# Block-sorted attention and a gated MLP on one core: chunk 2's queries and two units of chunk 1 transposed by DMA, a new order for the first two chunks

## The chip, the cores and the metric

The kernel runs on one core of a Trainium2 chip. The core has five engines that run side by side: TensorE (PE, matrix products, with its weight loads shown as PEld), VectorE (DVE), ScalarE (ACT), GpSimd (POOL) and SyncE (SP, which here only issues DMAs). Sixteen DMA engines move data between the memory of the chip and the core's own memory, and inside the latter. DMAs are put into queues by SP, ACT and POOL; loads that change the type from f32 to bf16 are issued by POOL here. Results of PE go to PSUM, a small memory of banks, and are copied out of it ("evicted") by DVE or ACT.

The metric is device time in microseconds (us), the median of several executions. One execution was recorded by the profiler; its span is the time from its first to its last instruction.

## The reference

For each of 4 batches and 8 heads, a net of 8x8 numbers is normalized five times by rows and columns, and its result mixes the 8 blocks (96 rows each) of keys and values. Each block of 96 queries then attends to the mixed block of keys at its place. The attention output is reshaped to 3072 tokens of 512 numbers and goes through a two-layer MLP with the gate `h * cos(h)`.

```
for _ in range(5):
    P = exp(P - max(P, -1));  P = P / (sum(P, -1) + 1e-9);  P = P / (sum(P, -2) + 1e-9)
k_sorted = einsum('bhij,bhjcd->bhicd', P, k_blocks)      # 8 blocks of 96 rows, 64 wide
v_sorted = einsum('bhij,bhjcd->bhicd', P, v_blocks)
scores = (q_block @ k_sorted_block.T) / 8
attn = exp(scores - max);  attn = attn / (sum(attn) + 1e-9)
x = (attn @ v_sorted_block).transpose(0, 2, 1, 3).reshape(3072, 512)
h = x @ w_in                                             # 512 -> 2048
out = (h * cos(h)) @ w_out                               # 2048 -> 512
```

Inputs and output are f32; the products run in bf16.

## The kernel before

The tokens are worked in 8 **chunks** of 384: chunk n is batch n // 2 and one half (4 of 8 blocks) of its rows. A chunk has 4 **units**, one for each block of 96 rows; a unit is all 8 heads of it. Two batches make a **group**: chunks 0 to 3 are group 0, chunks 4 to 7 group 1.

A unit (n, u) goes through these steps. PE makes the scores of 8 heads (`s_ps` in chunks 0 and 1, `qk_products` later); DVE takes the maximum and subtracts it (`s_max`, `s_sub`, later `qk_reduce`); ACT takes the exponential into one of three buffers `p_buf` (`expo`). The probabilities are transposed into `pT` in one of two ways: with `on_pe=True` by 8 transposes on PE into PSUM (`p_ps`, name `pps`, L776) and a copy out of it (`p_ev`), without it by one DMA transpose that SP issues (L533). PE multiplies by the values (`av_products`), DVE divides by the sum (`av_norm`), and the result is transposed into `xT` (`x_ps`, `x_ev`). Then come the MLP's first product, the gate and the second product: for chunk 0 `up_four`, `cos_four`, `gate_four` and quarters `down_four` of 4 matmuls (names `h`, `c`, `gg`, `o`), from chunk 1 on `up` and `down`.

Ahead of the units, the keys and values are mixed on PE by block matrices `bds` and `bdv` made from the normalized net. Chunk 0's keys come from `kp`, the rest of group 0 from `ks`/`kse` (6 parts of 8 columns), group 1's from `k_sort_g` out of the tile `pair`. Half of the keys is needed on the other 64 partitions too: `k_swap` exchanges the halves by two DMAs of SP (L421, L422), for group 0 after the last `kse`, for group 1 after the last `k_next`. The scores of chunk 2 and of chunk 4 wait for it. The values are read through a copy `vperm` with permuted columns, made by POOL (`v_permute`, four instructions, L179), which needs all of the values' loads.

Queries come in two forms. For chunks below `NQ = 3` one load (L119) brings 4 rows at a time, PE transposes them (`q_products`, name `qps`, L268: 16 transposes for each half of the heads) and DVE or ACT places them in `q_turned`; rows of x then stand in another order, which `x_transpose` undoes with `order`. From chunk `NQ` on, eight small loads (L129) bring them into a tile with zeros between the heads (`zeros_between`, L137), `q_mem` for even chunks and a part of `kv` for odd ones, and two DMA transposes of SP turn them (`q_transpose_dma`, L149).

The order on every engine is the order in which the program is written, so the list of calls behind `k_next` and `w_two` (L845 and below) decides it by hand, engine by engine; an engine that waits holds up all that stands behind it. POOL issues the loads and also does the permutations and zeros; with some loads it waits first: `hold_keys` waits for the exchange of the keys, `p_hold(2, 2)` for a transposed `pT`. POOL's loads use eight completion semaphores in turn, so a ninth load waits for the first to land. SP issues stores, exchanges and transposes in the order of the list. Some functions take `fill`: so many matmuls of zeros that keep PE busy and whose result is overwritten.

Around the end of chunk 1 the list reads (L1036 to L1052, some calls left out):

```
    ks(1, *B)
    ...
    kse(1, A)
    k_swap(kT[1])
    q_transpose(2, 0, (V, V), *C)
    q_transpose(2, 1, (V, V), *B)
    zeros_between(3)
    load_q(3)
    hold_keys()
    load_pair(vbuf, vin_d, 0 * CD // 6, 1 * CD // 6)
    ...
    up(1, 0)
    v_sort_b(1, 0, 8, A, *C)
```

## Time and profile before

| | |
|---|---|
| median of 3 runs | 236.1 us (234.94 to 236.75) |
| the profiled execution, its own time | 235.54 us |
| its span, first to last instruction | 233.6 us, 1.9 us less than its time |
| PE busy | 224.1 us (96% of the span) |
| VectorE, ScalarE, GpSimd busy | 171.0, 154.4, 95.9 us |
| granted clock of PE | 1.00 throughout |
| moved by DMA | 31.19 MB in 67672 packets |

A row of the view in order of time has the start and the length in us, the engine, the line, the operation, the tiles as out<-in, the sizes and the count, and in brackets the idle time of the engine before it with what ended it. Matmuls are pipelined and their ends are modelled, so the time of a group is better read from the starts of neighbouring rows. A row of DMA issues has the tiles, the queue that issued, the count, the KB of one and the median time from issue to landing in us. A row of windows has the stretch and its length, the busy time of PE, PEld, DVE, ACT and POOL with counts, the granted clock, the DMA engines' busy share and the GB/s that they wrote.

### The profile page before, as it was taken

What the parts mean: (1) busy time and instruction counts of PE and PEld (TensorE: products, weight loads), DVE (VectorE), ACT (ScalarE), POOL (GpSimd) and SP (SyncE); (2) the same over time, 40 slices, a digit from 0 to 9 for tenths busy, and PEclk for the clock granted to TensorE, in tenths of its full rate; (3) what the DMA queues carried; (4) which work ended last, traced back from release to release, by engine and by line L of the source; (5) the groups of instructions that cost most, each with busy time, mean ns of one, the idle gap of its engine ahead of it and who ended that gap; (6) DMA issues with size and microseconds to landing.
All of it is one profiled execution on the core that took longest, in us unless ns stands there. A gap on an engine that the chain in (4) does not pass through costs nothing.

```text
span 233.6 us, 5420 instructions
## 1 busy us (share of the span) xinstructions
PE 224.1 (96%) x2212; PEld 141.8 (61%) x2212; DVE 171.0 (73%) x291; ACT 154.4 (66%) x209; POOL 95.9 (41%) x121
## 2 busy tenths in 40 slices
PE   8778999999999999998999999999999999999994
PEld 3367899567665656655666546655665566556553
DVE  6769867987789867885498885997699769745700
ACT  5648886776889758795788565655665566816621
POOL 7999999399950093992609002600000000000000
PEclk9999999999999999999999999999999999999999
DMA  5999999993999799898999679934933360351012
GB/s 73 227 190 206 203 206 227 204 223 124 124 134 175 123 166 151 130 198 134 139 145 101 96 99 195 170 65 88 177 128 64 73 186 0 68 144 45 3 45 90
DMA packets 67672, 31.19 MB, mean 134 GB/s; under 512 B 56384, under 2 KB 63168, under 8 KB 67392
## 3 DMA queue, kind: packets, MB, share of 16 engines
q0 software_dynamic: 24048, 13.64, 43.3%
q1 hardware_dynamic: 43312, 17.02, 35.1%
q8 instruction: 17, 0.28, 0.5%
q10 hardware_dynamic: 288, 0.20, 0.3%
q14 instruction: 7, 0.06, 0.1%
HBM read 27.27 MB, written 6.29 MB: 144 GB/s over the span
## 4 chain that ended last, share of the span: by engine, by line
PE 82%; DMA 8%; DVE 3%; POOL 3%; ACT 1%; issue 1%; SPq 0%; ACTq 0%; DVEq 0%; POOLq 0%
PE h L614 30%; PE o L639 27%; DMA kv<-in_v_dram 5%; PE h L798 5%; PE o L819 4%; PE sc L438 4%; PE av L570 3%; POOL vperm L179 3%; DMA pT<-p_buf 2%; PE ks L408 2%; PE o L1167 2%; DMA kTs<-kTs 1%; DVE xn L583 1%; PE vs L458 1%; PE pps L776 1%
## 5 line engine op out<-in xcount | busy, mean ns | idle before, releaser
L614 PE MATMUL h<-xT,w_in_t 128*128 128x384 bf16 x448 | 78.4, 326 | 0.0
L639 PE MATMUL o<-w_out_t,gg 128*128 128x512 bf16 x320 | 76.3, 379 | 0.0
L622 DVE TENSOR_TENSOR gg<-c,h 128x768 bf16<-128x768 f32 x56 | 52.7, 949 | 19.5 <-ACT c L618 19.4
L618 ACT ACTIVATE c<-h,half_pi 128x768 f32<-128x768 f32 x56 | 50.4, 900 | 24.5 <-PE h L614 23.6
L614 PEld LDWEIGHTS <-w_in_t 128*128 128x128 bf16 x448 | 42.2, 98 | 26.3 <-DVE xT L259 0.3
L639 PEld LDWEIGHTS <-gg 128*128 128x128 bf16 x320 | 29.1, 99 | 27.8
L515 ACT ACTIVATE p_buf<-s 96x768 bf16<-96x768 f32 x32 | 26.7, 842 | 5.6 <-DVE s L489 4.7
L179 POOL COPY vperm<-kv 64x768 bf16<-64x768 bf16 (+2 forms) x12 | 28.4, 2408 | 4.4 <-DMA kv<-in_v_dram 4.4
L489 DVE TENSOR_TENSOR s<-sc,mx 96x384 f32<-96x384 f32 (+1 forms) x33 | 24.3, 736 | 1.6
L487 DVE TENSOR_REDUCE mx<-sc 96x4 f32<-96x384 f32 (+1 forms) x33 | 24.0, 728 | 0.0
L583 DVE TENSOR_TENSOR xn<-av,r 96x512 bf16<-96x512 f32 x32 | 22.0, 687 | 1.1
L129 POOL DMA_DIRECT2D kv<-in_q_dram x24 | 16.0, 677 | 0.8 <-issue 0.5
L438 PE MATMUL sc<-kTs,q_turned 128*128 128x96 bf16 x224 | 15.4, 206 | 0.3 <-DMA kTs<-kTs 0.3
L257 ACT CAST kTs<-ks 128x512 bf16<-128x512 f32 x20 | 11.3, 582 | 6.3 <-PE ks L408 5.3
L581 DVE RECIPROCAL r<-av 96x8 f32<-96x8 f32 x32 | 6.4, 199 | 12.0 <-PE av L570 11.8
L438 PEld LDWEIGHTS <-q_turned 128*128 128x128 bf16 x224 | 12.6, 98 | 4.0 <-DVE s L489 0.6
L257 ACT COPY kv<-o 128x512 f32<-128x512 f32 (+2 forms) x10 | 5.2, 523 | 14.1 <-PE o L639 11.5
L129 POOL DMA_DIRECT2D q_mem<-in_q_dram x16 | 10.7, 690 | 4.6 <-DMA kv<-in_v_dram 4.2
L819 PE MATMUL o<-w_out_t,gg 128*128 128x512 bf16 x48 | 11.7, 379 | 0.0
L259 DVE COPY kv<-o 128x512 f32<-128x512 f32 (+1 forms) x5 | 3.1, 611 | 11.1 <-PE o L1167 8.5
L798 PE MATMUL h<-xT,w_in_t 128*128 128x192 bf16 x128 | 11.1, 246 | 0.0
L798 PEld LDWEIGHTS <-w_in_t 128*128 128x128 bf16 x128 | 10.5, 98 | 0.0
(128 smaller groups left out, 276.9 us busy)
## 6 DMA issues: line engine op xcount, KB each, us to landing
out_dram<-kv SPq DMA_DIRECT2D x12, 256.0 KB, 2.6
out_dram<-o_s SPq DMA_DIRECT2D x10, 256.0 KB, 3.7
w_in_t<-in_moe_w_in_dram POOLq DMA_DIRECT2D x4, 512.0 KB, 11.6
w_out_t<-in_moe_w_out_dram POOLq DMA_DIRECT2D x4, 512.0 KB, 12.6
kv<-in_k_dram POOLq DMA_DIRECT2D x2, 768.0 KB, 10.0
kv<-in_v_dram POOLq DMA_DIRECT2D x2, 768.0 KB, 13.3
pair<-in_k_dram POOLq DMA_DIRECT2D x2, 768.0 KB, 12.3
kv<-in_v_dram POOLq DMA_DIRECT2D x6, 256.0 KB, 5.6
```

Source lines behind the costliest of these rows:

```text
L129: nc.gpsimd.dma_start(out=q_heads[:, i, :, e], in_=src[:, ih * IC + i, :, e])
L179: nc.gpsimd.tensor_copy(dst, src)
L438: nc.tensor.matmul(out, q_of(n, hp)[:, x:x + 128], keys_of(n, u, h2, hp), start=True, stop=True)
L487: nc.vector.reduce_max(mx[:], scv, axis=AX.X)
L489: nc.vector.tensor_tensor(s, scv, mx.to_broadcast(list(s.shape)), op=ALU.subtract)
L515: nc.scalar.activation(p[:, :, :blk], s_t.pop((n, u)).rearrange("p e h c -> p (e h) c"), AF.Exp, scale=scale)
L583: nc.vector.tensor_tensor(xn.rearrange("p h e d -> p e h d"), avv[:, :, :, :D], r.to_broadcast([blk, 2, H2, D]), op=ALU.mult)
L614: nc.tensor.matmul(h[:, f2, :w], w_in_t[:, kk, f * 128:(f + 1) * 128], xT[n][:, kk], start=(kk == 0), stop=(kk == KC - 1))
L618: nc.scalar.activation(c[:], h[:, :, :w], AF.Sin, bias=half_pi[:, 0:1])
L622: nc.vector.tensor_tensor(gt[n, fp // 2][:, f:f + 2], c[:], h[:, :, :w], op=ALU.mult)
L639: nc.tensor.matmul(o[:], gt[n, f // 4][:, f % 4, ts * 128:(ts + 1) * 128], w_out_t[:, f, :], start=(f == 0), stop=(f == FC - 1))
L798: nc.tensor.matmul(o[:, part, f2 * w:(f2 + 1) * w], w_in_t[:, kk, f * 128:(f + 1) * 128], xT[0][:, kk, h * w:(h + 1) * w], start=(kk == 0) ...
```

## The change

Four things are changed, all in one list of calls.

- `NQ` is 2 instead of 3. Chunk 2's queries come by the eight small loads into `q_mem` and are turned by two DMA transposes; their 32 transposes on PE and four copies on DVE go. The zeros in `q_mem` are now laid for chunk 2 (`zeros_between(2)`) instead of chunk 4, whose call goes, as does `z_turned(0)`. Chunk 2's rows of x are in plain order. The place of `pT` for unit 0 of chunks 3 and 4 is kept by writing the numbers 3 and 4.
- Units (1, 1) and (1, 0) have `expo` without `on_pe`: SP transposes their probabilities, and two `p_ps` and `p_ev` go.
- The two loads of `pair` stand behind three of the four permutations of the second batch's values. `hold_keys` and the first three of six loads of group 1's values move behind `p_hold(2, 2)`, next to the other three.
- The order of the first two chunks is written anew: the first stage's key and value products, the fills, chunk 0's `down_four` behind those of the token tiles 1 and 2, the key parts `ks` spread through chunk 1 with `ks(0)` last, and the load of the sine table (`sine_next`) ahead of chunk 1's `up`.

```diff
-    QR, NQ = 4, 3
+    QR, NQ = 4, 2
...
-        if u == 0 and n in (NQ, NQ + 1):
+        if u == 0 and n in (3, 4):
...
+    q_products(1, 0, 0, 16, *C)
+    zeros_between(2)
+    cos_four(1, 0)
+    load_q(2)
...
+    v_permute(slice(64, 128), hi=48)
     load_pair(pair, kin_d, 0 * CD // 2, 1 * CD // 2)
     load_pair(pair, kin_d, 1 * CD // 2, 2 * CD // 2)
-    v_permute(slice(64, 128))
+    v_permute(slice(64, 128), 48)
...
+    expo(1, 1)
...
+    expo(1, 0)
...
+    q_transpose_dma(2)
...
+    ks(0, *B)
     down_four(0, 2)
...
+    kse(0, V)
+    k_swap(kT[1])
     x_ev(1, 1, A)
+    sine_next()
     x_ps(1, 0, *B)
     x_ps(1, 3, *B)
...
+    down_four(0, 3)
+    down_out(0, A)
     zeros_between(3)
     load_q(3)
-    hold_keys()
-    load_pair(vbuf, vin_d, 0 * CD // 6, 1 * CD // 6)
-    load_pair(vbuf, vin_d, 1 * CD // 6, 2 * CD // 6)
-    load_pair(vbuf, vin_d, 2 * CD // 6, 3 * CD // 6)
...
-    zeros_between(4)
...
     p_hold(2, 2)
-    for z in range(3, 6):
+    hold_keys()
+    for z in range(6):
         load_pair(vbuf, vin_d, z * CD // 6, (z + 1) * CD // 6)
     load_q(4)
```

What stands on POOL between chunk 0 and the loads of chunk 3's queries, before (`pair` are group 1's keys, `kv<-in_q_dram` chunk 3's queries, `vperm<-kv` the permutation of the second batch's values):

```order
L685 MEMSET p_buf_108 96x8x32
L685 MEMSET p_buf_109 96x8x32
L119 DMA q_mem<-in_q_dram 96x8x256
L92 DMA pair<-in_k_dram 128x3072 x2
L179 COPY vperm<-kv 64x1536 x4
L137 MEMSET kv 96x16x64 x2
L129 DMA kv<-in_q_dram 96x4x64 x8
```

The same place on POOL after the change:

```order
L685 MEMSET p_buf_108 96x8x32
L685 MEMSET p_buf_109 96x8x32
L137 MEMSET q_mem 96x16x64 x2
L129 DMA q_mem<-in_q_dram 96x4x64 x8
L179 COPY vperm<-kv 64x1536 x3
L92 DMA pair<-in_k_dram 128x3072 x2
L179 COPY vperm<-kv 64x1536
L137 MEMSET kv 96x16x64 x2
L129 DMA kv<-in_q_dram 96x4x64 x8
```

The one query load has become two memsets and eight loads, and the pair loads stand behind three permutations instead of ahead of all four.

SP from the start of the program to the transposes of chunk 3's queries (`q_turned_95<-kv`), before; the exchange of the keys is the pair L421 and L422:

```order
L81 DMA P<-in_sort_net_dram 32x64
L629 DMA out_dram<-o_s 128x512 x2
L629 DMA out_dram<-c 128x512
L421 DMA kTs<-kTs 64x1536
L422 DMA kTs<-kTs 64x1536
L149 DMA_TRANSPOSE q_turned_95<-kv 128x16x96 x2
```

And after:

```order
L81 DMA P<-in_sort_net_dram 32x64
L533 DMA_TRANSPOSE pT<-p_buf_108 128x8x96
L629 DMA out_dram<-o_s 128x512
L533 DMA_TRANSPOSE pT<-p_buf_107 128x8x96
L149 DMA_TRANSPOSE q_turned_94<-q_mem 128x16x96 x2
L629 DMA out_dram<-c 128x512
L421 DMA kTs<-kTs 64x1536
L422 DMA kTs<-kTs 64x1536
L629 DMA out_dram<-o_s 128x512
L149 DMA_TRANSPOSE q_turned_95<-kv 128x16x96 x2
```

Four transposes have come in ahead of the exchange, and one store has moved behind it.

POOL at the loads of group 1's values, after the change (`kv<-in_v_dram` are the values, `q_mem<-in_q_dram` chunk 4's queries); before, the cast from `kTs` and three of the loads stood far ahead, behind chunk 3's queries:

```order
L541 CAST held<-pT 96x1
L426 CAST held<-kTs 128x1
L92 DMA kv<-in_v_dram 128x1024 x6
L129 DMA q_mem<-in_q_dram 96x4x64 x8
L179 COPY vperm<-kv 128x1536 x4
```

All six value loads now follow one another, and chunk 4's query loads and the permutation come behind them.

More of the change, by code (lines that the diff above doesn't have):

```diff
@@ L843, in w_two @@
         next(wz)
-    kp(2, *B)
-    kp(0, *B)
+    kp(2, *B, fill=1)
+    blocks.append(block([pick[:, :, z * PB:(z + 1) * PB] for z in (1, 0)]))
     v_permute(slice(0, 64), 32, False, 8, 40)
@@ L850 @@
     v_permute(slice(0, 64), 56, False, 8, 64)
-    k_place(2, A, 1)
-    k_place(2, V, 0)
+    k_place(2, A, 0)
+    k_place(2, V, 1)
     kp(1, *B)
+    values_matrix()
+    kp(0, *B)
+    k_place(1, V, 0)
+    v0(0, *C)
     k_place(0, A, 0)
-    blocks.append(block([pick[:, :, z * PB:(z + 1) * PB] for z in (1, 0)]))
-    k_place(1, V, 0)
-    k_place(1, A, 1)
-    values_matrix()
+    k_place(1, V, 1)
+    s_ps(0, 0)
+    v0e(0, A)
+    s_max(0, 0)
+    v0(4, *C, fill=1)
     k_place(0, A, 1)
-    s_ps(0, 0, fill=3)
@@ L906 @@
+    v0(3, *C, fill=1)
+    s_sub(0, 1)
+    v0e(7, A)
+    s_ps(0, 2, fill=1)
+    v0e(3, A)
+    p_ev(0, 0, V)
+    v0(1, *C)
+    kxp(0)
+    expo(0, 1, True)
+    s_max(0, 2)
+    v0e(1, A)
+    p_ps(0, 1, *B, fill=2)
+    kxp(1)
+    s_sub(0, 2)
+    p_ev(0, 1, A)
+    av_products(0, 0, fill=1)
+    kxp(2)
     z_turned(1)
     av_norm(0, 0, True)
+    p_ps(0, 3, *C, fill=3)
+    expo(0, 2, True)
     av_products(0, 1)
-    p_ev(0, 3, A)
-    p_ps(0, 2, *C)
     av_norm(0, 1, True)
     x_ps(0, 0, *B)
+    p_ev(0, 3, A)
@@ new lines @@
+    s_ps(1, 0)
+    s_sub(1, 2)
+    kse(5, A)
+    down_four(1, 3)
+    s_max(1, 0)
+    expo(1, 2, True)
+    ks(2, *B)
+    s_ps(1, 3)
+    down_four(2, 1)
+    kse(2, A)
+    s_sub(1, 0)
+    down_out(1, A)
+    down_four(2, 2)
+    s_max(1, 3)
+    expo(1, 0)
+    ks(4, *B)
+    p_ps(1, 2, *B)
+    s_sub(1, 3)
+    kse(4, A)
+    down_four(2, 3)
+    q_transpose_dma(2)
+    p_ev(1, 2, V)
+    expo(1, 3, True)
+    ks(1, *B)
+    ks(3, *C)
+    kse(1, V)
+    av_products(1, 1)
+    down_out(2, A)
```

212 lines of the change are left out of this document (75 added, 137 removed).

## The prediction

> **What bounds the kernel now.** I read the page first, then the list of PE's waits, then PE's instructions in order of time, and last the DMA issues and windows. The page gives PE nearly the whole span. A busy PE is not yet a PE at its peak, so the second look is at its waits, and the third at the spacing of its matmuls.
>
> ```profile
> PE 224.1 (96%) x2212; PEld 141.8 (61%) x2212; DVE 171.0 (73%) x291; ACT 154.4 (66%) x209; POOL 95.9 (41%) x121
> PE vs L726 <- POOL vperm L179: 1.3, 2, 0.7
> 28.57 3.47 PE L798 MATMUL h<-xT,w_in_t 128*128 128x192 bf16 x40
> ```
>
> The longest entry among PE's waits is 1.3 us, for the value permutation in the first stage. From the first `h` matmul at 28.57 on, groups follow each other without a gap, so there a matmul taken away is time taken away, and a wait put in is time put in. The next rows, PE from one chunk to the next, carry most of the sum. The time of a group is read from its start to the start of the next row, since the ends are modelled and overlap.
>
> ```profile
> 47.21 0.52 PE L776 MATMUL pps<-ident,p_buf 96*96 96x96 bf16 x8
> 47.57 1.89 PE L819 MATMUL o<-w_out_t,gg 128*128 128x512 bf16 x8
> ...
> 54.52 1.03 PE L819 MATMUL o<-w_out_t,gg 128*128 128x512 bf16 x4
> 55.39 0.34 PE L785 MATMUL xps<-order,xn 96*128 96x96 bf16 x4
> 55.56 1.10 PE L408 MATMUL ks<-bd,kv 128*128 128x64 bf16 x32
> 56.59 0.90 PE L268 MATMUL qps<-ident,q_mem 96*64 96x96 bf16 x32
> 57.42 1.47 PE L614 MATMUL h<-xT,w_in_t 128*128 128x384 bf16 x8
> 58.73 0.63 PE L448 MATMUL vs<-bdv,vperm 128*128 128x64 bf16 x16
> 59.20 1.47 PE L614 MATMUL h<-xT,w_in_t 128*128 128x384 bf16 x8
> 60.50 0.40 PE L448 MATMUL vs<-bdv,vperm 128*128 128x64 bf16 x8
> 61.17 0.33 PE L438 MATMUL sc<-kTs,q_turned 128*128 128x96 bf16 x4 [0.28 <-DMA kTs<-kTs]
> ```
>
> The reader is to see chunk 2's first scores at 61.17, held for the exchange of the key halves (`k_swap`). Sixteen `vs` take 0.47, so eight take 0.23 and PE was ready at 60.73: it lost 0.44.
>
> **What is removed.** The 32 transposes of chunk 2's queries: 57.42 - 56.59 = 0.83 us of PE. Two groups of eight transposes of chunk 1's probabilities: 2 x (47.57 - 47.21) = 0.72. Their evictions from PSUM (four on DVE, two on ACT) go too; neither engine bounds this stretch, so I count them as nothing, and what covers them is PE's own stream. In all -1.55 us, if nothing is put in their place.
>
> **The first stage (to 28.57).** Here PE waits for others and only the order changes. I laid the new list against the old rows by hand. The second unit's scores now stand behind the value products `v0(5)`, whose last matmul needs the third piece of the permutation (the wait above), which makes them some 0.7 late. Against that, one transposed unit of x moves behind the first `h`. I take +0.2, with bounds of -0.8 and +1.0. The warm-up matmuls that are put at other places fill time in which PE waits.
>
> **The exchange of the key halves.** This is the wait that ended last before, so the question is when it lands now. It is issued by SP after the last key eviction. In the new list these matmuls of PE stand between that point and the scores: a quarter of `o` (55.39 - 54.52 = 0.87), two transposes of x (2 x 0.17), another quarter (0.87), two groups of `h` (2 x 1.30) and 24 `vs` (0.70). That is 5.4 us; taking off 0.9 for the eviction itself (0.67 for one of these casts and the hand-over, an estimate), some 4.5 us of cover, where the old list had 60.73 - 57.48 = 3.25. By itself that would remove the 0.44.
>
> But the pair keys' loads now run at that time:
>
> ```profile
> 39.97 1.10 POOL L92 DMA_DIRECT2D pair<-in_k_dram  x2
> 45.04 11.26 POOL L179 COPY vperm<-kv 64x1536 bf16<-64x1536 bf16 x4 [3.97 <-DMA kv<-in_v_dram]
> 56.54 1.83 POOL L137 MEMSET kv<- 96x1024 bf16 x2 [0.25 <-POOL vperm L179]
> 58.33 5.36 POOL L129 DMA_DIRECT2D kv<-in_q_dram  x8
> ```
>
> The order on POOL is now: zero `q_mem` (2 memsets, 1.83), load chunk 2's queries in the form of `load_q(3)` (8 issues, 5.36), three permutations (3 x 2.81 = 8.44), then the pair loads. The zeros wait for the last products from `q_mem`, which stand after as many `h` groups as before and end near 38.8. So the pair loads are issued at 38.8 + 1.8 + 5.4 + 8.4 = 54.4. The first values, for which POOL waited until 45.04, have landed when the permutation begins at 46.0. PE's work from those products to the last key eviction comes to about 15.1 us (ten quarters of `o` at 0.87 and the short groups), so with the eviction and 0.5 for waits on PSUM buffers and on the unit that comes by DMA the exchange is issued near 55.2. It goes out about 0.8 us behind the pair loads. What a transfer of SP does behind pair loads, the trace shows once:
>
> ```profile
> 46.66 3.79 SPq L629 DMA_DIRECT2D out_dram<-o_s  x2
> 57.48 0.54 SPq L421 DMA_DIRECT2D kTs<-kTs  x1
> out_dram<-o_s SPq DMA_DIRECT2D x1, 256.0 KB, 8.3
> out_dram<-o_s SPq DMA_DIRECT2D x1, 256.0 KB, 5.3
> kTs<-kTs SPq DMA_DIRECT2D x2, 192.0 KB, 2.9
> pair<-in_k_dram POOLq DMA_DIRECT2D x1, 768.0 KB, 10.4
> pair<-in_k_dram POOLq DMA_DIRECT2D x1, 768.0 KB, 14.3
> 46.00:50.00 4.00, 4.00 (x52) 2.63 (x49) 2.83 (x4) 3.15 (x7) 4.00 (x2) 1.00 1.05 216
> ```
>
> The two stores, issued at 46.66 and 50.11 (3.4 us apart), landed at 55.0 and 55.4, together with the second pair load (40.5 + 14.3 = 54.8), where the exchange with nothing large beside it took 2.9. The pair loads move 2 x 0.786 MB at the 216 GB/s of 46 to 50, thus 7.3 us after a start some 1.3 after issue: they end at 63.0. So the exchange lands between 58.9 (its 2.9 after the second issue, some 0.6 behind the first, near 56.0) and 64.3 (8.3 after it). I take **63.0**, with the pair loads, as the stores did. PE is ready at 60.73 - 1.55 + 0.2 + 0.5 = 59.9. It waits 3.1 us, and chunk 2's scores start at 63.0, 1.8 later than before. All that was gained is lost in this wait, and everything behind it moves by +1.8.
>
> One rule of the Trainium skill bears on this price ("DMA: Bandwidth & Descriptors", section "Queues, rings and completion order"): a DMA engine goes round the queues it has work for and drains a whole packet of some 9 to 17 descriptors before it turns to the next queue. By that the exchange would wait for the first pair load alone. The stores speak against it: the first pair load was in at 50.4, and the first store came 4.6 us after that. The time by it is the first rival.
>
> **The second group's values.** Six loads instead of three now follow the hold on POOL, with chunk 4's queries behind them.
>
> ```profile
> 81.68 1.60 POOL L92 DMA_DIRECT2D kv<-in_v_dram  x3 [0.27 <-issue]
> ...
> 92.22 0.67 POOL L129 DMA_DIRECT2D q_mem<-in_q_dram  x1 [3.59 <-DMA kv<-in_v_dram]
> 92.88 11.27 POOL L179 COPY vperm<-kv 128x1536 bf16<-128x1536 bf16 x4
> 83.00:87.00 4.00, 3.95 (x50) 2.48 (x49) 3.23 (x9) 1.88 (x3) 4.00 (x7) 1.00 1.00 142
> kv<-in_v_dram POOLq DMA_DIRECT2D x1, 256.0 KB, 9.2
> 94.42 3.58 SPq L149 DMA_TRANSPOSE q_turned<-q_mem  x2
> 98.09 1.13 SPq L421 DMA_DIRECT2D kTs<-kTs  x1
> 102.08 2.60 SPq L533 DMA_TRANSPOSE pT<-p_buf  x2
> kTs<-kTs SPq DMA_DIRECT2D x2, 384.0 KB, 4.8
> 105.91 0.50 PE L438 MATMUL sc<-kTs,q_turned 128*128 128x96 bf16 x8
> 107.01 0.43 PE L570 MATMUL av<-vS,pT 96*128 96x65 bf16 x8 [0.60 <-DMA pT<-p_buf]
> ```
>
> The reader is to follow one chain: the last query load waits on POOL until the last value load has landed (3.59 of idle, to 92.22); SP's transposes of these queries wait for that load (94.42); the big key exchange is queued behind them (98.09, the second half at 99.27), and behind it the probabilities (102.08). Six pieces of 0.262 MB at 142 GB/s take 11.1 us from 83.0, so the last value load lands at 94.1 instead of 91.9 (82.7 + 9.2); if the transpose that lay beside it before costs as much again, at 97. I take 95.2, thus +3.3 for the last query load, with bounds of 0 and +6. The exchange then ends near 99.3 + 3.3 + 5.1 = 107.7, and the scores at 105.91 need it: PE waits 1.8. The `av` that stood at 107.01 follows at 108.1, since its own old wait falls into the new one. That is **+1.1**, with bounds of 0 and +4. The value products have more room: their second group at 103.0 needs two permuted pieces, ready at 92.9 + 3.3 + 5.6 = 101.8.
>
> **The sum.** +1.8 at chunk 2's first scores (in it the -1.55), +1.1 at chunk 4's: +2.9 us. Behind 107 the list is as it was and PE streams. Against the profiled execution, 235.5 us, that is 238.4; the median of the runs shown, 236.1, lies 0.6 above that execution, so the forecast is **239.0**.
>
> **The rivals.**
> - *The exchange passes the loads.* If an engine drains one load's share and then the exchange, the first pair load ends at 54.4 + 1.3 + 0.786/0.216 = 59.3 and the exchange lands near 61.3: +0.1 there, +1.1 later, 237.3. For it: the stores moved nothing until the first pair load was in. Against it: they came no sooner than the second.
> - *The values cost nothing.* At 142 GB/s and with an early last query the chain moves by 2.2, about what it has in hand (SP is free at 99.9, the probabilities come at 102.1). Then +1.8 alone: 237.9.
> - *Neither wait comes: faster.* Its one mechanism is that the exchange gets ahead of the pair loads. It decides at 0.8 us: if PE reaches the last key eviction that much earlier, or POOL its third permutation that much later, the exchange lands at 58 to 59, inside its 4.5 us of cover. Then -1.55 + 0.7 - 0.44 = -1.3, and up to -2.8 with the good end of the first stage: 233.3 to 234.8.
> - *The transposed probabilities are late too.* SP's two transposes of queries that met value loads took 7.3 us each to land:
>
> ```profile
> q_turned<-kv SPq DMA_TRANSPOSE x2, 7.3
> ```
>
> Chunk 1's second such unit is issued near 48.6 by the sum above and used at 52.3, while chunk 2's query loads may still run. At 7.3 it lands at 55.9, PE waits 3.6, and the whole case comes to 241 to 243.
>
> **How the numbers follow.** Forecast with both waits 0.46 (own range 237.6 to 241); the exchange passes 0.14; values free 0.12; neither 0.16; late probabilities 0.12. Two runs of this kernel differ by up to 0.8%, so 1% is about what a measurement can tell. Faster by over 1% is below 233.7: most of the fourth case, 0.11. Slower by over 1% is above 238.5: four fifths of the first case, all of the last, a third of the values' case, 0.52. The rest is 0.37. The range leaves out the best end of the fourth case and the worst of the last: 234.0 to 242.0.
>
> **What would show it.** In the profile of the changed kernel: chunk 2's first scores (L438) with over 2 us of idle before them, ended by the exchange, and the pair loads issued ahead of it; a gap of 1 to 3 us at chunk 4's first scores or the `av` behind them; no `qps` beside those of chunks 0 and 1; the first `h` between 27.8 and 29.6. The forecast is wrong if the exchange lands in under 5 us, or if the last query load is issued less than 2 us later than before, measured from the hold.

## The result, and the profile after

The changed kernel takes **244.6 us** (median of 4 runs, 244.0 to 246.3) where the kernel before takes 235.9 (4 runs, 234.9 to 236.8): a ratio of 1.038, 95% interval 1.031 to 1.045. It is 8.7 us slower. The forecast was 239.0 with a range to 242.0: right in sign, too small in size. The profiled execution took 245.18, its span 243.3. Now and then an execution is some per cent longer than the others of the same kernel (one of e15 below took 266.0), and the ratios leave such executions out.

The page of the changed kernel, the engines' busy time and the clock that TensorE was granted in 40 slices of 6.1 us each:

```profile
PE 225.4 (93%) x2145; PEld 141.6 (58%) x2166; DVE 169.9 (70%) x289; ACT 153.1 (63%) x206; POOL 97.6 (40%) x124
...
PEclk9997999999769999999999999999999999999999
```

PE has 67 matmul records fewer (48 transposes are gone; a trace lacks some records), but is busy for 93% of a longer span, and the clock is down in the eleventh and twelfth slice (61 to 73 us) and, in the first stage, in the fourth (18 to 24 us). The list of PE's waits (us in total, times, longest) names the cause:

```profile
PE sc L438 <- DMA kTs<-kTs: 7.1, 2, 6.1
...
PE av L570 <- DMA pT<-p_buf: 0.8, 2, 0.5
```

Before, the wait of the scores for the exchange was 0.3. PE in order of time (start, us, what, idle time before it) shows the two places:

```profile
60.14 1.46 PE L614 MATMUL h<-xT,w_in_t 128*128 128x384 bf16 x8
61.44 0.40 PE L448 MATMUL vs<-bdv,vperm 128*128 128x64 bf16 x8
67.93 0.48 PE L438 MATMUL sc<-kTs,q_turned 128*128 128x96 bf16 x4 [6.09 <-DMA kTs<-kTs]
68.21 2.76 PE L614 MATMUL h<-xT,w_in_t 128*128 128x384 bf16 x8
...
71.08 1.46 PE L614 MATMUL h<-xT,w_in_t 128*128 128x384 bf16 x8
...
115.27 0.50 PE L438 MATMUL sc<-kTs,q_turned 128*128 128x96 bf16 x8 [0.99 <-DMA kTs<-kTs]
116.24 0.43 PE L570 MATMUL av<-vS,pT 96*128 96x65 bf16 x8 [0.47 <-DMA pT<-p_buf]
```

Chunk 2's first scores start at 67.93 instead of 61.17. The group of `h` behind them takes 2.55 from its start to the next row, where 1.30 is usual. Chunk 4's first scores start at 115.27 instead of 105.91. What POOL issued, in order of time:

```profile
41.93 5.39 POOL L129 DMA_DIRECT2D q_mem<-in_q_dram  x8
47.37 8.46 POOL L179 COPY vperm<-kv 64x1536 bf16<-64x1536 bf16 x3
55.78 1.11 POOL L92 DMA_DIRECT2D pair<-in_k_dram  x2
...
101.16 1.34 POOL L129 DMA_DIRECT2D q_mem<-in_q_dram  x2 [1.76 <-issue]
```

The same of SP's queue:

```profile
57.49 0.54 SPq L421 DMA_DIRECT2D kTs<-kTs  x1
58.08 0.78 SPq L422 DMA_DIRECT2D kTs<-kTs  x1
```

The list of DMAs has their time from issue to landing (median of two):

```profile
pair<-in_k_dram POOLq DMA_DIRECT2D x2, 768.0 KB, 10.8
...
kTs<-kTs SPq DMA_DIRECT2D x2, 192.0 KB, 8.6
```

One by one in the trace: the pair loads landed at 64.5 and 69.2 (8.8 and 12.9 after issue), the halves of the exchange at 65.0 and 67.8 (7.5 and 9.8). Before, an exchange took 2.9.

Where the 9.6 us between the two profiled spans lie, by these marks of PE's stream: the first `h` is 1.26 later; from there to chunk 1's second `h` stage PE is 0.30 faster (28.55 for 28.85); from there to chunk 2's first scores 5.80 slower (9.55 for 3.75); from these to chunk 3's first scores (86.00, before 77.79) 1.45 slower (18.07 for 16.62), of which 1.25 is the slow `h`; from there to chunk 4's first scores 1.15 slower (29.27 for 28.12); behind that 0.28.

### The profile page after: what moved, and what is told of

It is laid out like the page before. It is cut to its first block, busy times and chain, and to the rows that moved or that the text cites. A ratio compares the mean times of both kernels' runs of the same rounds, so it can differ in the third digit from the quotient of the medians.

```text
span 243.3 us, 5322 instructions
## 1 busy us (share of the span) xinstructions
PE 225.4 (93%) x2145; PEld 141.6 (58%) x2166; DVE 169.9 (70%) x289; ACT 153.1 (63%) x206; POOL 97.6 (40%) x124
## 4 chain that ended last, share of the span: by engine, by line
PE 74%; DMA 14%; DVE 5%; POOL 2%; issue 2%; ACT 1%; SPq 0%; ACTq 0%; DVEq 0%; POOLq 0%
PE h L614 30%; PE o L639 25%; DMA pT<-p_buf 5%; DMA kv<-in_v_dram 5%; PE h L798 4%; DMA kTs<-kTs 4%; PE sc L438 3%; PE av L570 3%; DVE xn L583 2%; POOL vperm L179 2%; PE o L1160 1%; PE ks L408 1%; PE vs L726 1%; PE vs L458 1%; PE xps L601 1%
## 5 line engine op out<-in xcount | busy, mean ns | idle before, releaser
L614 PE MATMUL h<-xT,w_in_t 128*128 128x384 bf16 x448 | 79.7, 330 | 0.0
L639 PE MATMUL o<-w_out_t,gg 128*128 128x512 bf16 x305 | 74.0, 379 | 0.8
L614 PEld LDWEIGHTS <-w_in_t 128*128 128x128 bf16 x448 | 42.5, 99 | 27.5 <-issue 1.8
L639 PEld LDWEIGHTS <-gg 128*128 128x128 bf16 x320 | 29.1, 99 | 27.9
L179 POOL COPY vperm<-kv 64x768 bf16<-64x768 bf16 (+2 forms) x12 | 28.5, 2416 | 0.6 <-DMA kv<-in_v_dram 0.5
L129 POOL DMA_DIRECT2D q_mem<-in_q_dram x24 | 16.2, 683 | 6.0 <-DMA kv<-in_v_dram 3.9
L581 DVE RECIPROCAL r<-av 96x8 f32<-96x8 f32 x32 | 6.3, 198 | 12.3 <-PE av L570 12.2
L257 ACT COPY kv<-o 128x512 f32<-128x512 f32 (+2 forms) x10 | 5.2, 524 | 14.3 <-PE o L639 11.7
L819 PE MATMUL o<-w_out_t,gg 128*128 128x512 bf16 x44 | 11.1, 379 | 0.2
L257 ACT CAST vS<-vs 96x512 bf16<-96x512 f32 x16 | 9.1, 582 | 3.1 <-PE vs L726 3.1
## 6 DMA issues: line engine op xcount, KB each, us to landing
w_in_t<-in_moe_w_in_dram POOLq DMA_DIRECT2D x4, 512.0 KB, 11.3
w_out_t<-in_moe_w_out_dram POOLq DMA_DIRECT2D x4, 512.0 KB, 12.3
pair<-in_k_dram POOLq DMA_DIRECT2D x2, 768.0 KB, 10.8
```

Of the source, the lines that this page charges most:

```text
L129: nc.gpsimd.dma_start(out=q_heads[:, i, :, e], in_=src[:, ih * IC + i, :, e])
L179: nc.gpsimd.tensor_copy(dst, src)
L257: eng.copy(dst, src)
L614: nc.tensor.matmul(h[:, f2, :w], w_in_t[:, kk, f * 128:(f + 1) * 128], xT[n][:, kk], start=(kk == 0), stop=(kk == KC - 1))
L639: nc.tensor.matmul(o[:], gt[n, f // 4][:, f % 4, ts * 128:(ts + 1) * 128], w_out_t[:, f, :], start=(f == 0), stop=(f == FC - 1))
```

## The experiments

In "before" and "changed" below, the two kernels are meant. A run's time is a median; the ratio is to the kernel before on the same chip.

| run | us | before | ratio, 95% interval |
|---|---|---|---|
| e2 before, pair loads late | 243.6 | 236.0 | 1.032, 1.024 to 1.040 |
| e1 changed, pair loads behind the exchange | 240.3 | 236.0 | 1.017, 1.010 to 1.024 |
| e3 changed, PE kept busy in the wait | 245.0 | 236.0 | 1.039, 1.031 to 1.047 |
| e4 changed, old first stage | 248.0 | 236.0 | 1.050, 1.040 to 1.059 |
| e10 before, new first stage | 235.9 | 235.4 | 1.004, 1.002 to 1.006 |
| e6 before, values in one go | 241.9 | 235.4 | 1.027, 1.022 to 1.032 |
| e11 as e6, chunk 4's queries early | 235.6 | 235.5 | 1.002, 0.999 to 1.005 |
| e12 before, chunk 4's queries early | 237.7 | 235.5 | 1.010, 1.006 to 1.013 |
| e16 changed, chunk 4's queries early | 244.8 | 235.3 | 1.038, 1.032 to 1.044 |
| e18 before, e2 and e6 together | 250.1 | 235.3 | 1.060, 1.052 to 1.068 |
| e15, e20 changed, one pair load late | 243.2, 243.8 | 235.3, 235.2 | 1.034, 1.027 to 1.041 (e20) |
| e19 before, chunk 2's queries by DMA | 244.5 | 235.3 | 1.038, 1.032 to 1.043 |
| e17 changed, the two units by PE again | 247.2 | 235.2 | 1.052, 1.048 to 1.056 |
| e8 changed, pair loads ahead of chunk 3's queries | 245.8 | 235.4 | 1.045, 1.038 to 1.051 |
| e9 as e8, old first stage | 244.0 | 235.4 | 1.037, 1.033 to 1.041 |
| e13 changed, all three queues relieved | 241.2 to 245.8 | 235.5 | - |
| e14 as e13, old first stage | 242.3 | 235.5 | 1.026, 1.019 to 1.033 |

### Is it the pair loads beside the exchange? (e2, e1)

Two theories: the late pair loads hold the exchange (1), or SP's own queue does (2). e2 moves nothing but these loads, in the kernel before:

```
-    load_pair(pair, kin_d, 0 * CD // 2, 1 * CD // 2)
-    load_pair(pair, kin_d, 1 * CD // 2, 2 * CD // 2)
-    v_permute(slice(64, 128))
+    v_permute(slice(64, 128), hi=48)
+    load_pair(pair, kin_d, 0 * CD // 2, 1 * CD // 2)
+    load_pair(pair, kin_d, 1 * CD // 2, 2 * CD // 2)
+    v_permute(slice(64, 128), 48)
```

> The kernel before with one edit alone: the two pair loads stand behind three of the four permutations. Theory 1: the pair loads go out near 53.6, the exchange near 57.5 as before; it lands near 66, chunk 2's first scores move from 61.2 to about 66, and the time rises from 235.9 by 5 to 7 us (the wait, and slower matmuls after it). Theory 2: nothing was put into SP's queue, so the exchange lands in about 3 us and the time stays within 0.5 us.

PE of e2 in order of time:

```profile
60.98 0.40 PE L448 MATMUL vs<-bdv,vperm 128*128 128x64 bf16 x8
67.08 0.48 PE L438 MATMUL sc<-kTs,q_turned 128*128 128x96 bf16 x4 [5.70 <-ACT vS L257]
67.36 2.76 PE L614 MATMUL h<-xT,w_in_t 128*128 128x384 bf16 x8
...
70.36 2.43 PE L614 MATMUL h<-xT,w_in_t 128*128 128x384 bf16 x8
```

The wait is there with nothing else changed (the row names ACT, whose eviction was long done; the exchange landed at 66.3 and 66.9, 8.3 and 8.4 after issue). Here two groups of `h` are slow. Theory 1 holds, with 7.5 us where 5 to 7 were expected. (A store that SP had issued at 56.69, ahead of the exchange, has a part in it; more of that under e20.) e1 undoes this one part in the changed kernel:

```
     v_permute(slice(64, 128), hi=48)
-    load_pair(pair, ...)      # both
     v_permute(slice(64, 128), 48)
...
     load_q(3)
+    hold_keys()               # moved up from the values' loads
+    load_pair(pair, ...)      # both
     up(1, 0)
...
-    hold_keys()
```

> The changed kernel with the two pair loads moved behind the exchange of the keys and behind chunk 3's query loads (POOL waits for the exchange first). If the pair loads beside the exchange cost the time (theory 1), the exchange lands in 3 to 4 us, chunk 2's first scores start near 62 with less than 0.6 us of idle before them, the first h behind them takes 1.3 us instead of 2.55, and the time falls from 244.6 to about 237.5. If what delays the exchange is SP's own queue, the four transposes and the store put ahead of it (theory 2), the scores still wait over 3 us and the time stays over 241.

PE of e1:

```profile
59.52 0.33 PE L438 MATMUL sc<-kTs,q_turned 128*128 128x96 bf16 x4 [0.17 <-issue]
...
79.41 0.53 PE L570 MATMUL av<-vS,pT 96*128 96x65 bf16 x8 [3.34 <-DMA pT<-p_buf]
...
80.80 2.98 PE L639 MATMUL o<-w_out_t,gg 128*128 128x512 bf16 x8
```

and its SP queue:

```profile
65.76 10.55 SPq L149 DMA_TRANSPOSE q_turned<-kv  x2
76.41 3.90 SPq L533 DMA_TRANSPOSE pT<-p_buf  x3
```

The exchange lands in 3.2 and 3.8, and chunk 2's scores wait for nothing. 4.3 us are back, where some 7 were expected. The loads now lie beside the transposes of chunk 3's queries, which land 11 after issue, and SP issues chunk 2's probabilities only at 76.41, when it is done issuing those: PE waits 3.34 at `av`, and the `o` behind that is slow. The wait has moved one queue further.

### What the wait costs beside its own length (e3)

```
     v_sort_b(1, 16, 8, A, *C)
+    idle(26)      # 26 matmuls of no use
     qk_half(2, 0, 0, *C)
```

> The changed kernel with 26 matmuls of zeros (some 5.6 us) in PE's long wait ahead of chunk 2's first scores; they compute nothing that is used. If idle PE loses its clock and the first matmuls after the wait pay for it, the h behind the scores takes 1.3 instead of 2.55 us, the granted clock stays 1.00 from 60 to 70, and the time falls by 1.2 to 1.6 us to about 243.2. If the slow h has another cause (the DMAs in flight), nothing changes.

PE of e3:

```profile
59.43 5.82 PE L246 MATMUL idle<-warm 128*128 128x512 bf16 x26
65.73 0.33 PE L438 MATMUL sc<-kTs,q_turned 128*128 128x96 bf16 x4 [0.48 <-issue]
65.90 1.46 PE L614 MATMUL h<-xT,w_in_t 128*128 128x384 bf16 x8
67.20 0.40 PE L448 MATMUL vs<-bdv,vperm 128*128 128x64 bf16 x8
```

With PE kept busy the granted clock is 1.00 and `h` takes 1.30, so the slow `h` comes from the idle time before it. In this profile the stretch from chunk 2's to chunk 3's first scores is that of the kernel before (16.61 us, against 18.07 in the changed kernel). The median did not fall, though (245.0). That the slow clock counts in the time is thus read from the spacing of the matmuls and is not shown by the times.

### The first stage (e4, e10)

e4 puts the old list back into the changed kernel, up to the first `h`; e10 puts the new list into the kernel before.

> The changed kernel with the old list of the first stage, up to the first h of chunk 0 (the queries of chunk 1 in the new order). If the new order of the first stage costs time, the first h starts at 28.6 instead of 29.8 and the whole time falls by 1.2 us to about 243.4, as the pair loads and the exchange move by the same amount. If the loss is taken up by the wait for the exchange, the time stays at 244.6.

> The kernel before, with only the new order of the first stage (up to the first h, queries of the same unit as before). Theory 1 (the order itself makes the first h 1.26 later, as in the changed kernel): first h at 29.8, time 237.2. Theory 2 (it is late only with the other parts of the change, or what it loses is made up before chunk 2's scores, where PE lost 0.44): 235.9 to 236.4.

By its ratio e10 costs 0.4 to 1.5 us, by the medians 0.5. The first `h` stood at 28.57 in e10 and at 29.83 in the changed kernel, with the same list; over eight profiles of the new list it lies between 28.3 and 30.8, over ten of the old between 28.6 and 29.6. What parts them is PE's clock in the first stage. Windows of the kernel before and of the changed kernel (the figure before the last two is the granted clock):

```profile
20.00:25.00 5.00, 4.82 (x76) 4.43 (x77) 4.49 (x7) 4.43 (x9) 4.82 (x9) 1.00 1.30 204
20.00:30.00 10.00, 9.46 (x166) 7.69 (x165) 8.46 (x15) 7.95 (x13) 9.61 (x18) 0.84 1.28 205
```

In the changed kernel the clock was at 0.50 from 19.7 to 23.2. With such a stretch the first `h` comes at 29.8 to 30.8 in four profiles of the new list, and at 29.1 and 29.6 in two of the old; without one it comes at 28.3 to 28.6 in four of the new (mean 28.5) and at 28.6 to 28.9 in eight of the old (mean 28.7). So the new order costs nothing while the clock holds, and the 1.26 of the profiled run goes with the slow clock: both of e10's theories are too simple. Six of e10's ten executions have a mean clock of 0.992 or 0.993, which is what one stretch of 3.4 us makes (235.8 to 237.6 us; the other four 235.3 to 235.9), but only two of the thirteen of the kernel before beside it. The new order seems to bring the stretch on more often; why is not shown.

In e4 the first `h` came at 28.67, and chunk 2's scores only 0.6 earlier, at 67.33, since the exchange set them. Neither theory has the time (248.0): what made e4 slower lies behind, 49.9 instead of 47.3 to chunk 4's scores and 2.4 more up to the next `h`, as in e18 below.

### The second group's values (e6, e11, e12, e16)

e6 makes this one part of the change in the kernel before:

```
     load_q(3)
     hold_keys()
-    load_pair(vbuf, vin_d, ...)      # pieces 0, 1, 2
...
     p_hold(2, 2)
-    for z in range(3, 6):
+    for z in range(6):
         load_pair(vbuf, vin_d, z * CD // 6, (z + 1) * CD // 6)
     load_q(4)
```

> The kernel before, with one part of the change: the second group's values loaded in six pieces behind the hold, none early. Theory 1 (the values have a price of their own, by the queue of loads on POOL, SP's transposes of queries and the big key exchange): from the hold to the last query load 14.2 us as in the changed kernel instead of 11.0, the exchange of chunk 4's keys lands 1 to 3 us behind the point where PE wants it, time 237.0 to 238.7. Theory 2 (the wait of 1.0 at chunk 4's scores in the changed kernel is an after-effect of the wait at chunk 2's): 235.9, no wait at chunk 4's scores.

POOL of e6:

```profile
81.96 3.23 POOL L92 DMA_DIRECT2D kv<-in_v_dram  x6 [0.29 <-issue]
85.13 2.08 POOL L129 DMA_DIRECT2D q_mem<-in_q_dram  x3
...
93.33 1.42 POOL L129 DMA_DIRECT2D q_mem<-in_q_dram  x2 [4.80 <-DMA kv<-in_v_dram]
95.83 0.67 POOL L129 DMA_DIRECT2D q_mem<-in_q_dram  x1 [1.08 <-DMA kv<-in_v_dram]
97.30 0.67 POOL L129 DMA_DIRECT2D q_mem<-in_q_dram  x1 [0.80 <-DMA kv<-in_v_dram]
```

and PE:

```profile
109.88 0.50 PE L438 MATMUL sc<-kTs,q_turned 128*128 128x96 bf16 x8 [3.48 <-DMA kTs<-kTs]
110.70 0.43 PE L570 MATMUL av<-vS,pT 96*128 96x65 bf16 x8 [0.32 <-DMA pT<-p_buf]
110.97 1.82 PE L639 MATMUL o<-w_out_t,gg 128*128 128x512 bf16 x4
```

Alone, this part costs 6.6 us, more than theory 1 had (237.0 to 238.7). The last five query loads go out 0.3 after the landing of the load that stands eight before them on POOL (97.30 after the last value piece at 97.01); SP's transposes follow at 99.55, the big exchange at 103.25, and PE waits 3.5 for it and then runs slow. e11 takes the queries out of that queue and leaves the values in one go:

```
     zeros_between(4)
+    load_q(4)
...
-    load_q(4)
     expo(3, 0)
```

> The kernel before with the second group's values in one go (which alone came to 241.9), and chunk 4's queries loaded long before them, right after their buffer is zeroed. Theory 1 (the price of the values is that chunk 4's queries queue behind them, and the key exchange behind these): the exchange is issued near 98 instead of 103.3, no wait at chunk 4's scores, 235.4. Theory 2 (the value loads themselves cost: permutations late, transposes beside them slow): 238 to 242, with PE waiting for the permuted values or for a transpose near 101 to 106.

PE of e11:

```profile
108.30 0.61 PE L458 MATMUL vs<-bd,vperm 128*128 128x128 bf16 x8
108.75 0.50 PE L438 MATMUL sc<-kTs,q_turned 128*128 128x96 bf16 x8
109.09 0.42 PE L570 MATMUL av<-vS,pT 96*128 96x65 bf16 x8
```

No wait at these scores (one of 0.7, for the permuted values, stands 5 us ahead of them), and the time is that of the kernel before: the price of the values is the queue behind them. The same edit without the late values (e12) gains nothing:

> The kernel before, with only chunk 4's queries loaded early. Theory 1: the wait of 0.6 to 0.8 at chunk 4's scores and av goes, 234.6, and nothing else moves. Theory 2: the eight small loads meet the transposes of chunk 3's queries and of chunk 2's probabilities, which come 1 or more late: 236 to 238.

Its list of waits:

```profile
PE av L570 <- DMA pT<-p_buf: 2.0, 1, 2.0
```

Beside the eight small loads the transposes of chunk 3's queries land 9.4 and 12.3 after issue, and those of chunk 2's probabilities behind them 4.4 to 5.7, so PE waits 2.0 at chunk 2's first `av`: 237.7, theory 2. And in the changed kernel:

> The changed kernel with chunk 4's queries loaded right behind chunk 3's, not behind the values. Theory 1 (in the changed kernel the values cost only the wait of about 1.0 at chunk 4's scores): 243.6, no wait there. Theory 2 (the eight small loads make other transposes late, as in the kernel before, where they cost 2): 244.6 to 246.5.

The wait at chunk 4's scores is gone (28.12 from chunk 3's, as in the kernel before), and PE needs 0.8 less behind them, which the kernel before loses there too. But chunk 2's wait was 7.4 in its profile, and the time stays at 244.8. The price of the values in the changed kernel is thus small, some 1.2 by its trace, and not visible in the times.

### Do the two prices add up? (e18)

e18 is e2 and e6 in one kernel.

> The kernel before with the two late loads of the change and nothing else of it: the pair loads behind three permutations (alone 243.6) and the second group's values in one go (alone 241.9). Theory 1 (the two waits share one delay: once PE is late at chunk 2, the big exchange is that much less late for it): 244.5, PE's wait at chunk 4's scores about 1, as in the changed kernel. Theory 2 (the prices add up): 250.

The list of waits of e18:

```profile
PE sc L438 <- DMA kTs<-kTs: 10.2, 2, 7.0
```

Both waits are there in full (7.0 and 3.2), and 250.1 is the sum: 235.3 + 7.5 + 6.6 = 249.4. So theory 1 falls, and the changed kernel is 5.5 faster than its two late loads alone would make it. By the marks the two kernels reach chunk 2's first scores together (67.95 and 67.93). The difference lies behind them: the changed kernel takes 3.4 less to chunk 4's first scores and 2.1 less from these to the next `h`. Of the 3.4, 1.1 is a second slow `h` group in e18 alone, and 1.7 goes with this, that the third of chunk 2's transposed probabilities, for which the hold ahead of the values waits, lands 2.8 after issue and not 4.5. The 2.1 are slow clock: behind e18's wait of 3.2 the granted clock is 0.50 until 124.6, and behind the 0.99 of the changed kernel it stays at 1.00. Why that transpose lands sooner in the changed kernel was not tried.

### First load or all loads? (e15, e20)

```
     v_permute(slice(64, 128), hi=48)
     load_pair(pair, kin_d, 0 * CD // 2, 1 * CD // 2)
-    load_pair(pair, kin_d, 1 * CD // 2, 2 * CD // 2)
...
     load_q(3)
+    hold_keys()               # moved up from the values' loads
+    load_pair(pair, kin_d, 1 * CD // 2, 2 * CD // 2)
...
-    hold_keys()
```

> The changed kernel with only the second of the two pair loads moved behind the exchange (and behind chunk 3's queries). Theory 1 (the exchange lands with whatever is in flight ahead of it, so half the bytes, half the delay): second half of the exchange lands near 63.5 instead of 67.8, time 240.5 to 241.5, part of it lost again where the other half meets chunk 3's transposes. Theory 2 (by packets in turn, only the first load stands in the exchange's way): the exchange lands as before this edit, 65 and 67.8, time 244.6.

> The changed kernel with only the second pair load moved behind the exchange, once more, for a profile that can be compared (three of the four earlier times were 242.6 to 243.2, 1.4 below the changed kernel). Theory 1 (the exchange lands with all that is in flight ahead of it): the second half of the exchange near 63.5, PE waits about 2 there, and the rest of the gain goes to chunk 3's transposes beside the other pair load. Theory 2 (only the first load is in its way): it lands at 65 and 67.8, PE waits 6.

PE of e20:

```profile
61.63 0.40 PE L448 MATMUL vs<-bdv,vperm 128*128 128x64 bf16 x8
67.75 0.48 PE L438 MATMUL sc<-kTs,q_turned 128*128 128x96 bf16 x4 [5.73 <-DMA kTs<-kTs]
```

With half the bytes ahead of it the exchange landed no sooner: at 67.1 and 67.7, with the one load, which itself took 10.5 (56.75 to 67.2). So theory 1's half the delay for half the bytes falls, and theory 2's numbers come closer. By the trace's packets (the pieces that a transfer is cut into), 85 of the load and 9 of SP's queue started between 59 and 63 us; most of the exchange's came when the load's were through. The load's first 14 packets of 6,144 bytes took 1.46 us each on average, the later ones mostly 0.5 to 0.7. Why it starts so slowly is open.

With one load ahead, e20 cannot tell whether the exchange waits for the first load or for all of them. The packets of the other traces can. In the changed kernel the exchange's first packet started at 61.9, when most of the first load was through, and from 62 to 67 the engines started 137 packets of the second load and 126 of the exchange: the exchange waits for the first load and shares with the second. In e2 it landed 6.4 behind the first load (in at 59.9), since the store that SP had issued ahead of it took that place: the store's packets started from 60.3, the exchange's from 64.0. In e16 such a store, issued 0.4 ahead of the loads, shared with the first load itself from 58 on, and the exchange came behind it. So SP's own order has a part in the delay too.

### The removed work by itself (e19, e17)

e19 takes only the removal of the 32 query transposes into the kernel before, with the pair loads right behind the queries:

```
+    zeros_between(2)
+    load_q(2)                 # in eight pieces, behind q_products(1, 1)
...
     kse(4, A)
+    q_transpose_dma(2)
...
-    q_transpose(2, 0, (V, V), *C)
-    q_transpose(2, 1, (V, V), *B)
```

> The kernel before with one part of the change, the removal: chunk 2's queries zeroed, loaded in eight pieces and turned by DMA; pair loads directly behind them, all else in the old order. Theory 1 (the 0.83 of PE comes through): 234.6 to 235.0. Theory 2 (what replaces it is late: the pair loads are issued 5 to 6 later, and the transposes of queries and the exchange lie beside them until about 60): PE waits 1 to 3 at chunk 2's scores, 236 to 238.

SP of e19:

```profile
47.71 10.95 SPq L149 DMA_TRANSPOSE q_turned<-q_mem  x2
...
60.19 0.54 SPq L421 DMA_DIRECT2D kTs<-kTs  x1
```

The stretch of PE without the transposes is 0.65 shorter. But the two DMA transposes beside the pair loads landed 13.1 and 6.5 after issue, SP was held until 58.7, and the exchange went out at 60.19 instead of 57.48: PE waits 5.2, and the time is 9.2 us worse. Of the 8.2 by which its profile is longer, 4.5 lie ahead of chunk 2's first scores and 2.9 between these and chunk 3's, where the clock is at first down. The queries by DMA and the pair loads at their old place do not go together. e17 gives the two units of probabilities back to PE in the changed kernel:

```
-    expo(1, 1)                # and expo(1, 0)
+    expo(1, 1, True)          # p_ps and p_ev of both units put ahead of av
```

> The changed kernel with the two units of chunk 1's probabilities turned by PE again. Theory 1 (their 0.72 of PE work is taken from time in which PE waits for the exchange anyway): no difference, 244.6, the exchange landing at 65 to 68. Theory 2 (PE's work before the exchange counts): 0.7 more, or, since two stalls of 0.7 and 0.5 on the late transposes go, 0.5 less.

247.2, that is 2.6 more than the changed kernel, where 0.7 was the most expected. In its profile chunk 2's scores are even 1.4 earlier (66.53, since the pair loads were issued 1.5 earlier), and what it lost came behind them, in a second slow `h` (2.09) and around chunk 4. So PE's share before the exchange did not decide, and the price has no single place.

### Versions meant to relieve all queues (e8, e9, e13, e14)

e8 holds the pair loads until the exchange is in, puts them ahead of chunk 3's queries, and loads three value pieces early; e9 adds the old first stage. e13 puts them behind chunk 3's queries with chunk 4's queries behind them, and chunk 3's transposes behind chunk 2's probabilities; e14 adds the old first stage.

```
# e8
+    hold_keys()
+    load_pair(pair, ...)      # both
     zeros_between(3)
     load_q(3)
+    load_pair(vbuf, ...)      # pieces 0, 1, 2
...
-    hold_keys()
-    for z in range(6):
+    for z in range(3, 6):
# e13 (each call is moved from its old place)
     load_q(3)
+    hold_keys()
+    load_pair(pair, ...)      # both
+    load_q(4)
...
     expo(2, 2)
+    q_transpose_dma(3)
...
     k_sort_g(12, A, *B)
+    qk(3, 0)
```

> The changed kernel, with the pair keys' loads held until the exchange has landed and put ahead of chunk 3's queries, and with three of the six value pieces loaded early again, behind chunk 3's queries. Theory 1 (the transfers that collided cost the time): the exchange lands in about 3.5 us, the probabilities of chunk 2 no longer queue behind a late transpose of chunk 3's queries (3.3 us less than with the loads put behind those queries, 240.3), no wait at chunk 4's scores (1.0 less): 236.0. Theory 2 (each place of these loads meets some transpose or transfer that PE needs): 238 to 241, with a new wait of over 2 us on a DMA.

> The kernel of the run before it in this batch, with the first stage in the old order up to the first h. Theory 1 (the first stage of the change costs 1.3 us, and the 1.55 us of PE taken away come through when nothing waits): 1.3 less than that run, 234.7, first h near 28.6. Theory 2 (what the first stage gains is taken up by the wait for the exchange, as when it was undone in the changed kernel alone): as that run or slower.

> The changed kernel, with the pair loads behind the exchange, chunk 4's queries loaded right behind them, and chunk 3's transposes of queries issued behind chunk 2's probabilities (chunk 3's first scores a quarter of o later). Theory 1 (the change costs by three queues: the exchange behind the pair loads, chunk 2's probabilities behind a slow transpose, the big exchange behind the last query load): all three waits go, 240.3 - 3.3 - 1.2 = 235.8. Theory 2 (bandwidth: whatever stands beside 1.5 MB of pair loads is late): PE waits 2 or more for the probabilities or for chunk 3's queries, 238 to 241.

> The kernel of the run before it in this batch, with the old order of the first stage. Theory 1: 1.0 less than that run, since then nothing waits for a transfer and PE's own stream sets the time: 234.8. Theory 2 (a wait for a transfer still ends last): as that run.

The longest wait of e8:

```profile
PE av L570 <- DMA pT<-p_buf: 10.4, 1, 10.4
```

The waits of e14:

```profile
PE av L570 <- DMA pT<-p_buf: 3.2, 1, 3.2
...
PE sc L438 <- DMA q_turned<-kv: 1.0, 1, 1.0
```

In all four, chunk 2's scores wait for nothing, and the time is lost at the next transposes: in e8 the queries' transposes meet the early values (10.5 and 10.3 to land) and the probabilities stand behind them; in e14 the probabilities themselves lie beside the pair loads and chunk 4's queries and take 6.0 to 6.9. Each place tried for these 1.5 MB costs some DMA that PE waits for. The old first stage gave 1.9 in e9; e13's runs lie too far apart to say it of e14. Theory 1 falls in all four, and the times lie over the 238 to 241 that theory 2 gave for e8 and e13. No version beat the kernel before; e11 equals it.

## Why the prediction was wrong in size

**The chain was right.** Chunk 2's first scores wait for the exchange, which was issued behind the late pair loads (1.7 us behind, 0.8 forecast). e2 and e1 show it from both sides. No `qps` stands beside those of chunks 0 and 1.

**The removal** came out as forecast on the mean. -1.55, with +0.5 for buffers and the late unit, makes -1.05 for the stretch from the first `h`: in nine profiles with the changed middle list it is 27.5 to 28.6, mean 27.9, against 28.85, so -1.0. In the profile that was compared it is -0.30. There the transposed probabilities were late, a mild form of the last rival; PE in order of time:

```profile
51.90 0.43 PE L570 MATMUL av<-vS,pT 96*128 96x65 bf16 x8 [0.29 <-DMA pT<-p_buf]
...
52.83 0.56 PE L776 MATMUL pps<-ident,p_buf 96*96 96x96 bf16 x8 [0.50 <-ACT p_buf L515]
```

The second of these waits is for ACT, which had itself waited 1.4 for a buffer until the first unit's transpose landed, 6.0 after issue.

**The first stage**, +0.2 with bounds of -0.8 and +1.0: some -0.1 by the profiles in which the clock holds, inside the bounds; +1.26 in the profiled run, outside them, with the clock at 0.50 for 3.4 us. The forecast had no term for that.

**The step that failed is the exchange's landing**, "they end at 63.0" and "I take 63.0, with the pair loads". The loads' end was worked out as their bytes by the 216 GB/s of 46 to 50 us from a start 1.3 after issue. They landed at 69.2, the exchange at 67.8; PE waited 6.1 instead of 3.1, and chunk 2's scores moved by 6.8 instead of 1.8. The windows of the changed kernel (the last figure is GB/s):

```profile
58.00:62.00 4.00, 3.84 (x43) 2.44 (x41) 1.12 (x2) 2.96 (x7) 3.94 (x4) 1.00 0.85 150
62.00:66.00 4.00, 0.00 (x0) 0.00 (x0) 0.95 (x1) 1.07 (x2) 4.00 (x7) 0.76 1.04 244
66.00:70.00 4.00, 2.07 (x10) 1.21 (x11) 1.11 (x2) 0.00 (x0) 0.76 (x2) 0.50 1.55 209
```

The rate was lower at first, and from 62 on it was shared with the exchange. e20 shows that bytes are not the measure: a single load took 10.5. Why the loads start slowly stays open. The rows of before had a nearer price: the second pair load took 14.3 from its own issue there. The forecast quoted that row and then used a rate, of a window in which the pair loads alone moved, in its place. (54.9 + 14.3 gives the 69.2 to the digit, but by luck: the load was issued 1.4 later and took 12.9, and 11.3 to 13.6 in the other runs with the exchange beside it.)

**The rule it set aside had the order right.** The Trainium skill ("DMA: Bandwidth & Descriptors", section "Queues, rings and completion order") has an engine drain one packet, a group of some 9 to 17 descriptors, before it turns to the next queue. The forecast took from it that the exchange waits for the first load alone. The changed kernel agrees: the first half came 0.5 behind the first load, and the second 2.8 later, sharing with the second load. The stores of the kernel before, which the forecast held against the rule, agree too. From 46.7 to 50.1 none of their packets started; from 50 to 52, with the first pair load in, 54 did, beside 57 of POOL's. They landed with it because they shared with it, not because they waited for it. But the time given for that rival, a first load in at 59.3, failed by the same step as the forecast: it was in at 64.5. And in e16 a store shared with the first load itself, so the order is not settled for all cases.

**The slow clock was not in the sum.** By the windows the granted clock was 0.50 from 64.1 to 70.9 in the changed kernel, and PE lost 1.45 us behind its wait; in e16, with a wait of 7.4 and the clock down until 74.7, it lost 2.8. The clock fell in a wait of 2.5 (e4, at chunk 4) as well as in one of 6, and not in those of 2.0 (e12) and 1.0. Wherever it falls after the first 7 us, it is down for 3.4, 6.8 or 10.2 us at a time, so the cost hangs on where in that time the wait ends: the changed kernel's wait ended 3.0 us before the clock came back, e2's 5.3. The Trainium skill has this ("TensorE: Matmul & The Clock Gate", section "Part 1: The HAM clock gate"): half rate after an idle window of about 3.4 us, full after a busy one. One, two and three times 3.4 fit that; the wait of 2.5 in e4 is shorter than such a window.

**The values** came out as forecast in the changed kernel, partly by luck. From the hold to the last query load 14.2 us instead of 11.0, +3.2 where +3.3 was forecast. From chunk 3's first scores on, chunk 4's came 1.15 later, where 1.8 was forecast, and the `av` behind them 1.0 later, where 1.1 was. Alone (e6) the same step is +4.8 and the price 6.6, over the bound of +4: by its trace 3.6 to chunk 4's scores and 1.4 of slow clock behind them. The sum for the changed kernel, from the marks, is then: first stage +1.26, removal -0.30, wait +5.80, clock +1.45, values +1.15, the rest +0.28, together 9.64.

## What to carry to other kernels

To price a transfer that is put beside another, start from the time from issue to landing of the same transfer in the trace, and not from its bytes by a rate; here that was nearer, and still off by 1.4 us. Look at when a queue's packets start, too: two transfers that land together may have shared or waited. Follow the queue further than the first wait: here every place that was tried for one pair of loads made the next transpose or exchange late, and put into the kernel before, two late loads cost as much as the sum of their prices (e18). A wait of some 2.5 us or more on PE cost 1.4 to 2.8 us beyond its length here, since the clock is down behind it.

## What was not expected of the hardware

- A DMA transpose of SP that lies beside loads of POOL took 6.5 to 13.1 us to land (e1 11.3 and 10.8, e8 10.5 and 10.3, e12 9.4 and 12.3, e19 13.1 and 6.5), where it takes 4.0 to 4.5 alone. Since SP issues in order, what stands behind it waits as well.
- One load of 0.79 MB beside the exchange took longer (10.5 us, e20) than the first of two (8.8 in the changed kernel, 6.7 to 9.7 in the other runs with the exchange beside it).
- The first `h` came between 28.3 and 30.8 us with one and the same list, by whether the clock fell in the first stage, so that a single pair of profiles could not price it.
